# A linear-attention and GLU kernel: another hand-written order for its first stage, weight folds on halves of the array, and numerators that stand together

## The chip, the cores and the metric

The kernel runs on one core of one Trainium2 chip. The metric is the device time of one execution in microseconds (us). The five engines are named as in the profile: PE (matrix products; PEld is its weight loads), DVE, ACT and POOL (element-wise work), SP (which issues the DMA transfers).

## The reference

```python
xn = layernorm(x)                                   # x: 2048 x 1024, float32
q, k, v = split(xn @ wqkv)                          # 32 heads of 32
phi(t) = concat(softmax(t @ w_phi), softmax(-(t @ w_phi)))     # per head
num = phi(q) @ (phi(k).T @ v);  den = phi(q) @ sum(phi(k)) + 1e-6
s = concat_heads(num / den) @ wo
g = silu(((sigmoid(xn @ w_gate)) * (xn @ w_up)) @ w_down)      # inner width 3584
out = x + s * g
```

## The kernel before, in words

All large products are float32. An operand is split into a high and a low part, and a product is three matmuls of 128x128 by 128x512 (`mm3`, L224, L225, L226): high by high, high by low, low by high. Above that, each matrix product is cut into 2x2 blocks and made of seven block products, named B11, T2, T3, B21, T1, T4 and B22, whose operands are sums and differences of blocks. Those sums are made by POOL and DVE, the splits by ACT (the high part, L219 and L917) and DVE (the low part, L220 and L920), and PE is meant never to wait for them.

The tokens are worked in two halves of 1024. For each half come the projections V, K and Q (seven block products each; an `op` is one of them, four banks u of 48 matmuls in all), then 28 units of gate and up products (`glu`). Then follow the down projection (`dsteps`) and, for eight pairs of token tiles (`tp_`), the attention's output.

**The first stage** (L995, L996 and their neighbours) makes V for the first half. Its order is written by hand in the table `FIRST`: each entry is one small step, and `turn()` keeps each step behind the step ahead of it. `x0a`, `x0b`, `x1` and so on load a token tile; `bn`, `ag`, `add`, `sqrt`, `c`, `apply` are its layer norm; `T` transposes it on PE (L978); `V0a`, `r01` load weights; `xcast`, `xsub`, `wcast`, `wsub` are splits; `mm` are the matmuls (L996); `f` and `fc` are folds.

**A fold** multiplies the K or Q weights by `w_phi`, so that the projection gives t @ w_phi at once. There are eight groups, (K, 0) to (K, 3) and (Q, 0) to (Q, 3). A group loads four raw blocks n (`fold_load`, L323, 256 KB each), makes 16 matmuls with a block-diagonal `bd` (`fold_products`, L329, 128 rows by 128 columns, 128 columns moved; the profile has two records for each), copies the result out of the banks (`fold_copy`, L337 and L339), stores three of its blocks to `wf_d` (`fold_keep`, L350), loads the next group's raw blocks, and stores four sums. The first three groups stand in `FIRST`; the other five are in the queue `side`, and one is taken by `step()` after each bank u of the projections. The operands of the K and Q projections are read back from `wf_d` (L469, 1024 KB each).

**x tiles.** While the first half's gate products run, `x_task` prepares the second half's token tiles: it loads one, normalises it, stores it in pieces to `xs_d` (L665), loads it back in another order (L667), waits three steps (`yield`), transposes it on DVE (L672, which waits for that load) and, for every second tile, makes eight POOL pieces of sums (`x_sums`, L79). A step is one piece of background work, run after a block product.

**Numerators** (`numerators`, L832): for each pair `tp_`, 16 small matmuls of 64 columns and 256 moved columns, two records each, in two column halves of the array. They read `units_ph`, which DVE transposes (L817), and are called 13 products into the pair ahead.

Within an engine the framework's scheduler orders the instructions by its own estimate of times, unless `tc.issue_after(i)` puts an instruction behind another one. SP issues DMAs in order, and an SP instruction that waits holds up all that stand behind it.

Of the kernel before, what the change touches and what calls it, by code (L numbers as in the profile page):

```python
# [17 lines left out]
P = 128  # L18
# [14 lines left out]
class Ring:  # L33
# [3 lines left out]
    def next(self):  # L37
        self.n += 1
        return self.items[(self.n - 1) % len(self.items)]
# [56 lines left out]
x1, bn 1 0, x0a, bn 1 1, x0b, bn 0 0, wphi, x3, diag 1, ag 1, add 1, bn 0 1, sqrt 1, diag 0, ag 0, r01, add 0, c 1  # L96
0, sqrt 0, c 1 1, diag 2, c 1 2, r00, c 0 0, diag 3, c 0 1, c 0 2, c 0 3, V0a, f 0 1 3, c 0 4, c 0 5, apply 0 D, f 0
0 0, bn 3 0, r03, wcast B11 0, c 1 3, T 0 0 1, V0b, c 1 4, c 1 5, T 0 1 2, fc 0 1, wsub B11 0, xcast 0 0, fc 0 0,
r02, mm B11 0 0 a, xsub 0 0, xcast 0 1, f 0 3 3, V1b, apply 1 D, wcast B11 1, xsub 0 1, T 1 0 0, copy 0 0, V1a, mm
B11 0 0 b, bn 3 1, wcast B21 1, wsub B11 1, T 1 1 1, x2, copy 0 1, mm B11 0 1 a, xcast 1 1, ag 3, mm B11 0 1 b, copy  # L100
1 1, V2, bn 2 0, copy 1 0, f 0 2 2, bn 2 1, xcast 1 0, ag 2, mm B11 1 0 a, xsub 1 0, add 23, mm B11 1 0 b, xsub 1 1,
sqrt 23, wcast B21 0, x4, c 23 0, c 23 1, mm B11 1 1 a, c 23 2, c 23 3, evac B11 0, mm B11 1 1 b, c 23 4, c 23 5,
wsub B21 0, apply 2 A, x5, mm B21 0 0 a, bn 4 0, fc 0 3, T 2 0 0, V3, evac B11 1, T 2 1 1, bn 4 1, mm B21 0 0 b,
apply 3 A, ag 4, wsub B21 1, mm B21 1 0 a, xcast 2 1, mm B21 1 0 b, xcast 2 0, v 3 0 0 P, x6, copy 2 0, xsub 2 0, T
3 1 3, v 3 0 1 P, mm B11 2 0 a, bn 5 1, xcast 3 1, x7, mm B11 2 0 b, v 3 0 2 P, xsub 2 1, copy 2 1, v 3 0 3 P, fc 0
2, bn 6 0, mm B11 2 1 a, r10, mm B11 2 1 b, bn 7 1, v 3 1 0 P, r11, bn 5 0, v 3 1 1 P, T 3 0 2, kp 0, mm B21 0 1 a,
ag 5, xcast 3 0, v 3 1 2 P, bn 6 1, mm B21 1 1 a, copy 3 1, f 1 0 0, ag 6, xsub 3 0, v 3 1 3 P, f 1 1 1, r12, xsub 3
1, k 0 0 P, fc 1 0, bn 7 0, r13, k 0 1 P, mm B21 0 1 b, r20, ag 7, add 4567, mm B11 3 0 a, sqrt 4567, copy 3 0, mm
B11 3 0 b, c 4567 0, c 4567 1, v 2 0 0 D, evac B21 0, c 4567 2, c 4567 3, mm B21 1 1 b, c 4567 4, c 4567 5, apply 4
D, apply 7 A, mm B11 3 1 a, v 2 0 1 D, T 4 1 3, v 2 0 2 D, evac B11 2, v 2 0 3 D, T 4 0 2, v 2 1 0 D, copy 4 1, mm  # L110
B11 3 1 b, v 2 1 1 D, copy 4 0, apply 5 D, evac B21 1, f 1 3 3, xT3 0 0 D, fc 1 1, xT3 0 1 D, xT2 0 0 D, f 1 2 2,
evac B11 3, xT2 0 1 D, scast t3 0, xT4 0 0 D, xT4 0 1 D, T 5 0 0, fc 1 3, ssub t3 0, T 5 1 1, apply 6 A, kp 1, mm
B21 3 0 a, v 2 1 2 D, v 2 1 3 D, mm B21 2 0 a, v 0 0 0 D, v 0 0 1 D, copy 5 0, mm B21 2 0 b, k 0 2 D, copy 5 1, v 0
0 2 D, v 0 0 3 D, vst 3, mm B21 2 1 a, fc 1 2, v 0 1 0 D, T 6 1 1, k 0 3 D, scast t2 0, v 0 1 1 D, T 6 0 0, v 0 1 2
D, copy 6 1, mm B21 3 0 b, v 0 1 3 D, copy 6 0, xT3 1 0 D, xT3 1 1 D, wcast T2 1, T 7 0 2, xT3 2 0 D, xT3 2 1 D,
r21, mm B21 3 1 a, xT2 2 0 D, scast t3 1, mm B21 2 1 b, ssub t2 0, r22, wcast T2 0, v 1 0 0 D, r23, f 2 0 0, xT2 2 1
D, ssub t3 1, evac B21 2, vst 0, mm T2 0 0 a, scast t2 2, k 0 4 D, T 7 1 3, k 0 5 D, wsub T2 0, mm B21 3 1 b, copy 7
1, f 2 3 3, v 1 0 1 D, ssub t2 2, f 2 1 1, xT2 1 0 D, xT2 1 1 D, v 1 0 2 D, copy 7 0, mm T2 2 0 a, v 1 0 3 D, wcast
T3 0, v 1 1 0 D, mm T2 2 0 b, xT3 3 0 D, xT3 3 1 D, xT2 3 0 D, mm T2 2 1 a, scast t3 3, xT4 1 0 D, mm T2 0 0 b,
scast t2 1, xT2 3 1 D, v 1 1 1 D, scast t2 3, xT4 1 1 D, f 2 2 2, wsub T2 1, evac B21 3, scast t3 2, mm T2 0 1 a, fc  # L120
2 2, ssub t2 3, mm T2 3 0 a, fc 2 3, mm T2 2 1 b, ssub t2 1, fc 2 0, ssub t3 2, wcast T3 1, mm T2 3 0 b, k 1 0 D,
xT4 3 0 D, mm T2 0 1 b, scast t4 0, v 1 1 2 D, v 1 1 3 D, fc 2 1, wsub T3 0, V4, mm T2 3 1 a, scast t4 1, mm T2 1 0
a, mm T2 1 0 b, k 1 1 D, xT4 2 0 P, evac T2 2, mm T2 1 1 a, ssub t3 3, mm T2 3 1 b, k 1 2 D, ssub t4 1, mm T3 2 0 a,
k 0 6 P, evac T2 3, mm T2 1 1 b, xT1 1 0 D, mm T3 2 0 b, xT1 0 0 D, k 1 3 D, kp 2, wcast T4 0, k 1 4 D, mm T3 3 0 a,
xT4 3 1 D, xT4 2 1 P, evac T2 0, mm T3 3 0 b, wsub T3 1, scast t4 2, mm T3 2 1 a, vst 2, wcast T4 1, mm T3 0 0 a, k
# [5 lines left out]
D, mm T4 1 1 a, ssub b22 1, mm T4 2 0 b, xT1 0 1 D, scast t1 0, mm T4 2 1 a, wcast T1 1, mm T4 3 0 b, ssub t1 0, k 2  # L131
2 D, mm T4 3 1 a, scast t1 1, k 2 3 D, k 2 4 D, mm T4 2 1 b, scast t1 2, wsub T1 1, scast t1 3, mm T4 3 1 b, k 2 5
D, k 2 6 D, mm T4 1 1 b, ssub t1 2, k 2 7 D, ssub t1 3, ks 2, evac T4 3, ssub t1 1, wsub T1 0, evac T4 1, evac T4 2,
evac T4 0
"""


@with_exitstack
def hedgehog_glu_kernel(
# [74 lines left out]
    def pair(i):  # L214
        return slots[i][:, 0], slots[i][:, 1]
# [1206 lines left out]
```

## Time and profile before

| | |
|---|---|
| median of 3 runs (lowest, highest) | 2351.0 us (2350.98, 2352.16) |
| the profiled execution, and its span | 2350.23 us, 2348.5 us |
| busy: PE, DVE, ACT, POOL | 2331.4, 1624.6, 957.5, 1160.7 us |
| matmul records | 10644 |
| moved by DMA | 624.11 MB, mean 266 GB/s |

The span runs from the first to the last instruction. A matmul's own time (0.39 us for 512 columns) is longer than the step from one to the next (0.23 us), since matmuls overlap; so time is read here from start to start. In a row of a timeline the first number is the start, the second how long the merged row lasts, and what stands in brackets at the end is the idle time ahead of it, with what ended it.

### The profile page before, as it was taken

The numbers are of one execution on the slowest core, as the hardware profiler recorded it, in microseconds if no ns is written. First come the engines' busy times: TensorE is split into PE (matmuls) and PEld (weight loads), VectorE is DVE, ScalarE is ACT, GpSimd is POOL, SyncE is SP. The second block draws the span as 40 slices with busy tenths as digits, with TensorE's granted clock in tenths as the row PEclk, the third lists the DMA queues.
The fourth block names the chain that finished last, engine by engine and source line by source line (L and its number), as shares of the span: only waits on it lengthen the run. The fifth ranks groups of instructions, "written<-read, shape, count | busy, mean of one in ns | idle before, by whom it ended". The sixth has DMA issues, their size and how long they took to land.

```text
span 2348.5 us, 32142 instructions
## 1 busy us (share of the span) xinstructions
PE 2331.4 (99%) x10644; PEld 1922.2 (82%) x10644; DVE 1624.6 (69%) x2306; ACT 957.5 (41%) x1410; POOL 1160.7 (49%) x1320
## 2 busy tenths in 40 slices
PE   9999999999999999999999999999999999999999
PEld 7888888878888888888888888888888888887777
DVE  8734788677777675466867777866666777657655
ACT  7333354445454454233435344433434333344322
POOL 3210267677686642304363544555444455623777
PEclk9999999999999999999999999999999999999999
DMA  8875566888888889858888887879777877878774
GB/s 289 298 266 188 188 213 223 278 291 300 304 309 294 281 300 362 303 186 281 270 274 284 281 270 262 287 249 344 245 235 258 276 240 232 285 261 296 241 226 162
DMA packets 265415, 624.11 MB, mean 266 GB/s; under 512 B 36896, under 2 KB 65696, under 8 KB 260640
## 3 DMA queue, kind: packets, MB, share of 16 engines
q1 hardware_dynamic: 265248, 622.05, 78.0%
q8 instruction: 84, 1.38, 0.2%
q14 instruction: 83, 0.68, 0.1%
HBM read 373.42 MB, written 248.51 MB: 265 GB/s over the span
## 4 chain that ended last, share of the span: by engine, by line
PE 90%; DMA 4%; DVE 4%; issue 1%; ACT 1%; POOL 0%; SPq 0%; DVEq 0%; ACTq 0%
PE bank L224 29%; PE bank L225 29%; PE bank L226 29%; DMA fa<-w_down 2%; PE bank L602 1%; PE bank L832 1%; PE bank L329 1%; DMA x<-xk 1%; DVE x L920 1%; DMA fc<-xs_d 0%; DVE x L220 0%; DVE w L220 0%; DMA fa<-wv 0%; DVE w L920 0%; DMA wf_d<-x 0%
## 5 line engine op out<-in xcount | busy, mean ns | idle before, releaser
L225 PE MATMUL bank<-x,w 128*128 128x512 f32 x2352 | 916.4, 390 | 0.7 <-DVE x L220 0.7
L224 PE MATMUL bank<-x,w 128*128 128x512 f32 x2352 | 906.3, 390 | 3.7 <-DVE fc L1171 2.1
L226 PE MATMUL bank<-x,w 128*128 128x512 f32 x2352 | 905.9, 389 | 0.0
L79 POOL TENSOR_TENSOR fc<-fc 128x256 f32<-128x256 f32 x488 | 427.4, 907 | 480.0 <-DMA fc<-e_d 131.6
L220 DVE TENSOR_TENSOR w<-fa,w 128x512 fp32r<-128x512 f32 (+1 forms) x436 | 397.6, 915 | 201.3 <-ACT w L219 191.6
L219 ACT CAST w<-fa 128x512 fp32r<-128x512 f32 (+1 forms) x436 | 300.3, 691 | 556.8 <-PE bank L225 354.5
L224 PEld LDWEIGHTS bank<-x,w 128*128 128x128 f32 x2352 | 441.9, 188 | 97.1 <-DVE fc L1171 2.7
L225 PEld LDWEIGHTS bank<-x,w 128*128 128x128 f32 x2352 | 442.0, 188 | 92.7 <-DVE x L220 1.9
L226 PEld LDWEIGHTS bank<-x,w 128*128 128x128 f32 x2352 | 441.8, 188 | 91.8
L224 PE MATMUL bank<-w,x 128*128 128x512 f32 x636 | 248.4, 391 | 0.3 <-DVE fc L506 0.3
L225 PE MATMUL bank<-w,x 128*128 128x512 f32 x636 | 247.9, 390 | 0.0
L226 PE MATMUL bank<-w,x 128*128 128x512 f32 x636 | 247.4, 389 | 0.0
L79 POOL TENSOR_TENSOR fb<-fa 128x256 f32<-128x256 f32 x112 | 97.9, 894 | 218.6 <-PE bank L226 110.9
L79 POOL TENSOR_TENSOR fb<-fb,fc 128x256 f32<-128x256 f32 x132 | 123.6, 957 | 121.8 <-DVE fc L1188 121.6
L79 POOL TENSOR_TENSOR fc<-fc,sa 128x256 f32<-128x256 f32 x128 | 97.0, 788 | 93.5 <-issue 85.0
L224 PEld LDWEIGHTS bank<-w,x 128*128 128x128 f32 x636 | 119.4, 188 | 26.9 <-issue 1.9
L226 PEld LDWEIGHTS bank<-w,x 128*128 128x128 f32 x636 | 119.4, 188 | 24.8
L225 PEld LDWEIGHTS bank<-w,x 128*128 128x128 f32 x636 | 119.4, 188 | 24.3
L219 ACT CAST p<-fc 128x512 fp32r<-128x512 f32 x96 | 73.0, 764 | 131.2 <-DVE fc L575 79.0
L220 DVE TENSOR_TENSOR x<-fa,x 128x512 fp32r<-128x512 f32 x112 | 93.9, 839 | 45.0 <-ACT x L219 45.0
L219 ACT CAST w<-fb 128x512 fp32r<-128x512 f32 x112 | 69.0, 617 | 118.2 <-PE bank L225 86.4
L1188 DVE TENSOR_TENSOR fc<-fc,bank 128x512 f32<-128x512 f32 x84 | 57.5, 684 | 83.5 <-PE bank L226 61.6
(208 smaller groups left out, 2824.3 us busy)
## 6 DMA issues: line engine op xcount, KB each, us to landing
ws_d<-w SPq DMA_DIRECT2D x112, 512.0 KB, 4.2
w<-ws_d SPq DMA_DIRECT2D x112, 512.0 KB, 5.2
fa<-w_gu SPq DMA_DIRECT2D x84, 512.0 KB, 4.8
fa<-h_d SPq DMA_DIRECT2D x84, 512.0 KB, 4.9
fa<-wf_d SPq DMA_DIRECT2D x32, 1024.0 KB, 6.1
h_d<-fc SPq DMA_DIRECT2D x120, 256.0 KB, 4.7
fa<-w_down SPq DMA_DIRECT2D x80, 256.0 KB, 5.2
h_d<-fb SPq DMA_DIRECT2D x76, 256.0 KB, 4.5
```

Source lines behind the costliest of these rows:

```text
L79: last = self.engine.tensor_tensor(o[:, s], a[:, s], b[:, s], op=op)
L219: nc.scalar.copy(o[0], src)
L220: return nc.vector.tensor_sub(o[1], src, o[0].bitcast(F32))
L224: nc.tensor.matmul(o, a[0], b[0], start=first, stop=False, **kw)
L225: nc.tensor.matmul(o, a[0], b[1], start=False, stop=False, **kw)
L226: nc.tensor.matmul(o, a[1], b[0], start=False, stop=last, **kw)
L329: nc.tensor.matmul(ps[:, gs], r[:, gs], bd[:, 4 * (n // 2) + g], start=True, stop=True)
L602: nc.tensor.matmul(kvb[g // 2][:, g % 2 * 256:g % 2 * 256 + 256], v[:, g].rearrange("p a f -> p (a f)"), ph[:, g].rearrange("p a f -> p (a ...
L832: nc.tensor.matmul(ps[bs, j * 256:(j + 1) * 256], kv[:, 2 * j + b, bs], ph[:, 2 * j + b], start=True, stop=True, skip_group_check=True)
L920: nc.vector.tensor_sub(o[1], src, o[0].bitcast(F32))
L1188: v = nc.vector.tensor_add(b, u2 if q == 3 else u1, bank)
```

## The change

1. `FIRST` is another table: the tile x0 is loaded first, in halves, ahead of x1, and the steps behind it stand in another order.
2. `mm3` returns its last matmul. A list `last_mm` holds the last matmul of a row of them; the matmuls of the projections and of the attention's output, the later folds and the numerators are put behind it with `tc.issue_after`, so that they stand in the order of the code.
3. The five later fold groups are made by `fold_group`: the 128 rows are cut in two halves of 64, each half a matmul of its own (64 rows by 128 columns, 64 columns moved), alternately into two banks. They are copied by `fold_out`. The raw blocks of (K, 3) are loaded ahead of the loop over the operations, those of (Q, 0) by the fold of (K, 3). In `side` one or two empty steps stand ahead of each fold.
4. The 16 matmuls of `numerators` stand together.
5. `x_task` waits five steps in place of three, and counts 10 steps in place of 8.

```diff
 FIRST = """
-x1, bn 1 0, x0a, bn 1 1, x0b, bn 0 0, wphi, x3, diag 1, ag 1, add 1, bn 0 1, sqrt 1, diag 0, ag 0, r01, add 0, c 1
...
+x0a, x0b, bn 0 0, r02, bn 0 1, ag 0, x1, add 0, sqrt 0, c 0 0, c 0 1, c 0 2, c 0 3, r00, bn 1 0, c 0 4, wphi, bn 1
...
-        nc.tensor.matmul(o, a[1], b[0], start=False, stop=last, **kw)
+        return nc.tensor.matmul(o, a[1], b[0], start=False, stop=last, **kw)
...
+    def fold_group(which, k):
+        with tc.issue_after(last_mm[0]):
+            for n in range(4):
+                if n % 2 == 0:
+                    ps = [tps.next() for _ in range(2)]
+                r = folds.pop((which, k, n))
+                for g in range(4):
+                    for half in range(2):
+                        rs = slice(64 * half, 64 * half + 64)
+                        o = ps[half][:, n % 2 * 256:n % 2 * 256 + 256]
...
+                        m = nc.tensor.matmul(o, r[rs, g * P:(g + 1) * P], bd[rs, 4 * (n // 2) + g, rs], start=True, stop=True,
+                                             skip_group_check=True)
+                if n % 2:
+                    fold_out(which, k, n // 2, ps)
+        last_mm[:] = [m.ins]
...
-        for n in range(4):
-            fold_copy(which, k, n, fold_products(which, k, n, tps.next()))
+        fblock[which].next()
+        fold_group(which, k)
         fold_keep(which, k, False)
-        if k < 3:
+        if (which, k) != (Q, 3):
             for n in range(4):
-                fold_load(which, k + 1, n)
+                fold_load(*((which, k + 1) if k < 3 else (Q, 0)), n)
...
-        yield
-        yield
-        yield
+        for _ in range(5):
+            yield
...
+        with tc.issue_after(last_mm[0]):
+            for hb in range(2):
...
+                            m = nc.tensor.matmul(ps[bs, j * 256:(j + 1) * 256], kv[:, 2 * j + b, bs], ph[:, 2 * j + b],
+                                                 start=True, stop=True, skip_group_check=True)
...
+        last_mm[:] = [m.ins]
...
-    for w, k in [(K, 3)] + [(Q, k) for k in range(4)]:
+    for w, k, waits in ((K, 3, 2), (Q, 0, 1), (Q, 1, 2), (Q, 2, 2), (Q, 3, 2)):
+        side.extend([lambda: None] * waits)
         side.append(lambda w=w, k=k: fold(w, k))
+    for n in range(4):
+        fold_load(K, 3, n)
...
-    xs = [(8, lambda t=t: x_task(t)) for t in (CTT + 4 * a + q for q in range(4) for a in range(2))]
+    xs = [(10, lambda t=t: x_task(t)) for t in (CTT + 4 * a + q for q in range(4) for a in range(2))]
```

What it moves shows in the order of the built programs (line numbers of the changed kernel are larger by 3 to 47). First PE, in the middle of the attention's output: L832, in the changed kernel L867, are numerators, the rest products of three matmuls. Of one pair's 16, before, five stand at one place:

```order
L226 MATMUL bank_104<-x_0_90,fa_16054 128x512
L832 MATMUL bank_98<-fb_14626,p_14625 64x256 x4
L832 MATMUL bank_99<-fb_14626,p_14625 64x256
L224 MATMUL bank_102<-x_1_771,fa_16054 128x512
L225 MATMUL bank_102<-x_1_771,fa_16054 128x512
```

and eleven stand 51 matmuls later:

```order
L832 MATMUL bank_99<-fb_14626,p_14625 64x256 x3
L832 MATMUL bank_100<-fb_14626,p_14625 64x256 x4
L832 MATMUL bank_101<-fb_14626,p_14625 64x256 x4
L224 MATMUL bank_102<-w_93,x_1_611 128x512
L225 MATMUL bank_102<-w_93,x_1_611 128x512
```

After:

```order
L229 MATMUL bank_102<-w_93,x_0_91 128x512
L867 MATMUL bank_98<-fb_14710,p_14709 64x256 x4
L867 MATMUL bank_99<-fb_14710,p_14709 64x256 x4
L867 MATMUL bank_100<-fb_14710,p_14709 64x256 x4
L867 MATMUL bank_101<-fb_14710,p_14709 64x256 x4
L227 MATMUL bank_102<-w_93,x_0_91 128x512
```

So the five went to the place of the eleven. Pairs 4 to 8 stood as shown (five and eleven), pair 3 as one and fifteen, pair 2 as one, ten and five; each is one piece now. The first pair stands in three pieces, before and after.

Next SP's queue where the first stage ends. L323 (now L326) loads a raw block of a fold, L350 (now L385) stores a folded block, L469 (now L504) reads an operand of the K projection back, L503 (now L538) stores V. Before:

```order
L323 DMA fc_97<-wqkT 128x512
L323 DMA fb_96<-wqkT 128x512
L503 DMA qkv_d<-fc_97 128x512
L350 DMA wf_d<-fc_97 128x512 x2
L469 DMA fa_95<-wf_d 128x2048
L323 DMA fc_97<-wqkT 128x512
L350 DMA wf_d<-fc_97 128x512
L503 DMA qkv_d<-fc_97 128x512
L469 DMA fa_95<-wf_d 128x2048
```

After:

```order
L326 DMA fb_96<-wqkT 128x512 x2
L385 DMA wf_d<-fc_97 128x512 x2
L326 DMA fc_97<-wqkT 128x512
L504 DMA fa_95<-wf_d 128x2048 x2
L326 DMA fc_97<-wqkT 128x512
L385 DMA wf_d<-fc_97 128x512
```

The four L326 here are the raw blocks of (Q, 0). Both L504 now stand ahead of the last of them, and they wait for the landing of the two L385 above them, which are the folded blocks of (K, 3).

Last POOL, in the second unit of the gate products. `fc_97<-fc_97` are first the sums of the second x tile, and at the end (x2) a gate's product; `fa_95` are sums of the next unit's weights. Before:

```order
L79 TENSOR_TENSOR fc_97<-fc_97 128x256 x7
L79 TENSOR_TENSOR fb_96<-fa_95 128x256 x2
L79 TENSOR_TENSOR fc_97<-fc_97 128x256
L79 TENSOR_TENSOR fb_96<-fb_96,fa_95 128x256
L79 TENSOR_TENSOR fb_96<-fa_95 128x256
L79 TENSOR_TENSOR fb_96<-fb_96,fa_95 128x256
L79 TENSOR_TENSOR fb_96<-fa_95 128x256
L79 TENSOR_TENSOR fc_97<-fc_97 128x256 x2
```

After:

```order
L82 TENSOR_TENSOR fc_97<-fc_97 128x256 x6
L82 TENSOR_TENSOR fb_96<-fa_95 128x256 x2
L82 TENSOR_TENSOR fc_97<-fc_97 128x256 x2
L82 TENSOR_TENSOR fb_96<-fb_96,fa_95 128x256 x2
L82 TENSOR_TENSOR fc_97<-fc_97 128x256 x2
L82 TENSOR_TENSOR fb_96<-fa_95 128x256 x2
```

The gate's product stands two pieces further ahead. DVE's transpose of that x tile (L672, now L706) stands where it stood, behind the same bank's evacuation (L1169, now L1213).

127 lines of the change are left out of this document (74 added, 53 removed).

## The prediction

> **What bounds the kernel now.** I read the page first, then the busy time by stages, then the places where PE stands still.
>
> ```profile
> span 2348.5 us, 32142 instructions
> PE 2331.4 (99%) x10644; PEld 1922.2 (82%) x10644; DVE 1624.6 (69%) x2306; ACT 957.5 (41%) x1410; POOL 1160.7 (49%) x1320
> ...
> PE 90%; DMA 4%; DVE 4%; issue 1%; ACT 1%; POOL 0%; SPq 0%; DVEq 0%; ACTq 0%
> ```
>
> PE bounds it, and only two things can shorten the run: PE time per product, and the few places where PE waits. By stages (the first two numbers are a stage's length and PE's busy time in it):
>
> ```profile
> 0.00:20.00 20.00, 16.60 (x107) 15.27 (x107) 12.98 (x33) 10.74 (x20) 2.51 (x10) 1.00 0.94 334
> ...
> 60.00:80.00 20.00, 18.75 (x95) 15.73 (x94) 14.95 (x21) 5.04 (x8) 6.73 (x3) 1.00 0.91 325
> 80.00:100.00 20.00, 18.34 (x100) 15.49 (x100) 17.43 (x25) 9.65 (x17) 0.00 (x0) 1.00 0.64 213
> ...
> 440.00:500.00 60.00, 56.32 (x244) 45.52 (x243) 42.23 (x68) 23.82 (x35) 44.61 (x55) 0.99 0.82 276
> 500.00:2125.00 1625.00, 1625.00 (x7261) 1348.74 (x7261) 1147.27 (x1632) 675.97 (x982) 812.78 (x920) 1.00 0.82 277
> 2125.00:2348.00 223.00, 217.16 (x1045) 164.71 (x1043) 131.10 (x189) 66.76 (x115) 145.30 (x178) 1.00 0.70 231
> ```
>
> From 500 to 2125 us nothing is idle, and the change leaves the products there alone. What it can win or lose lies in the first 150 us, around 440 to 500, and after 2125. Its parts, by size:
>
> **Numerators in one piece.** Three pieces of the numerators, each between the last full matmul ahead and the first behind:
>
> ```profile
> 2170.17 0.39 PE L226 MATMUL bank<-w,x 128*128 128x512 f32 x1
> 2170.49 1.51 PE L832 MATMUL bank<-fb,p 128*64 128x256 f32 x10
> 2171.93 0.50 PE L224 MATMUL bank<-w,x 128*128 128x512 f32 x1
> 2172.26 0.39 PE L225 MATMUL bank<-w,x 128*128 128x512 f32 x1
> ...
> 2311.11 0.39 PE L226 MATMUL bank<-w,fa 128*128 128x512 f32 x1
> 2311.43 2.80 PE L832 MATMUL bank<-fb,p 128*64 128x256 f32 x22
> 2314.17 0.50 PE L224 MATMUL bank<-w,fa 128*128 128x512 f32 x1
> ...
> 2158.79 0.39 PE L226 MATMUL bank<-x,w 128*128 128x512 f32 x1
> 2159.11 2.38 PE L832 MATMUL bank<-fb,p 128*64 128x256 f32 x20
> 2161.42 0.50 PE L224 MATMUL bank<-x,x 128*128 128x512 f32 x1
> ```
>
> From full matmul to full matmul 10 records take 1.76 us, 22 take 3.06, 20 take 2.63. A record costs (3.06 - 1.76) / 12 = 0.108. A fixed cost is left beside the ordinary step of 0.23: 0.45 for 10 and for 22, 0.24 for 20. To each 0.10 is added, since the step behind a piece is 0.33 and not 0.23. So a piece costs 0.55 if its count of matmuls is odd (one is left without a partner in the other half), 0.34 if it is even. Before, six pairs have two odd pieces (1.10) and the second pair has odd, even, odd (1.44); after, each of the seven has one even piece. Sum: 6 x 0.76 + 1.10 = 5.7 us less. The piece stands where the later part stood, so what reads it is no later, and DVE's transposes for it were done by then. Bounds: 5.2 if the second pair's small piece costs less than this, 6.3 with a wait in that pair that may go too. **-5.7.**
>
> **Folds on halves of the rows.** One stretch of folds now, and the weight loads of both kinds:
>
> ```profile
> 134.15 1.05 PE L329 MATMUL bank<-fb,fc 128*128 128x128 f32 x8
> 135.04 1.95 PE L329 MATMUL bank<-fb 128*128 128x128 f32 x16
> 136.75 0.48 PE L225 MATMUL bank<-w,x 128*128 128x512 f32 x1
> ...
> L832 PEld LDWEIGHTS bank<-fb,p 128*64 128x64 f32 x256 | 18.6, 136 | 15.0 <-issue 5.6 <-DVE fb L817 1.6
> L329 PEld LDWEIGHTS bank<-fb 128*128 128x128 f32 x128 | 15.8, 191 | 2.2 <-issue 1.6
> ```
>
> 24 records take 2.60 us, 0.108 each, so a group of 32 takes 3.5. After, it has 64 records in 32 pairs. Each moves half the columns, but still loads 128 columns of weights. Column halves work side by side: 256 loads of 0.136 would be 34.8 us, and they cover 18.6. No row shows halves of the rows. A load's price is in the rows: 64 columns more cost 0.191 - 0.136 = 0.055, so 128 columns cost 0.11. That is what a fold record takes now, whichever of load and columns moved sets it. If the two halves' loads run side by side, as the column halves' do, a pair takes 0.11 and a group the same 3.5 as now. Halved price would be 0.054, serial loads 0.216: bounds of -8.6 and +17.3 for 160 pairs. I take the middle, since the loads' row is the nearest. Each group also enters and leaves the divided array, at the 0.34 of an even piece: five times. **+1.7.**
>
> [...]
>
> **The seam behind the first stage.** PE's three waits there:
>
> ```profile
> 78.40 1.13 PE L329 MATMUL bank<-fb 128*128 128x128 f32 x8 [1.25 <-DMA fb<-wqkT]
> ...
> 92.63 0.50 PE L224 MATMUL bank<-w,x 128*128 128x512 f32 x1 [0.34 <-DVE fc L506]
> 94.45 1.13 PE L329 MATMUL bank<-fb,fc 128*128 128x128 f32 x8 [1.32 <-DMA fc<-wqkT]
> ```
>
> With the 0.16 by which a matmul's own time exceeds the step, these are 1.4 + 0.5 + 1.5 = 3.4 us. Two are folds whose raw block had not landed. Now (K, 3) is loaded earlier and folded three banks later. **-3.4.** Behind it comes a new wait: the last raw block of (Q, 0) is queued on SP behind two 1024 KB reads that wait for stores to land.
>
> ```profile
> wf_d<-fc SPq DMA_DIRECT2D x3, 256.0 KB, 2.6
> ...
> GB/s 0 0 331 106 24 382 348 120 246 396 410 318 253 335 403 311 137 270 372 457 369 321 382 352 444 382 376 434 427 345 413 386 417 396 413 406 403 410 396 420
> ...
> wf_d<-fc SPq DMA_DIRECT2D x12, 256.0 KB, 6.1
> ```
>
> Count from the start of group (K, 3). It ends at 3.8. Two banks follow, 24 x 0.227 = 5.4; (Q, 0) starts at 9.3 and needs its last block at 12.1. The first half of (K, 3) is multiplied at 1.9, and copied and stored from 3.4 (estimated). The store lands 2.6 later (88 to 91 us, queue empty), at 6.0; the reads are issued then, the block's load at 7.0. The reads' 2.1 MB at some 410 GB/s take 5.1, behind 2.0 of delay, and the block 0.65: 13.8, a wait of 1.7. With a landing of 6.1 (88 to 112 us) it is 5.2; if the queue is faster, none. Late behind this wait on SP are the stores of V and (K, 3)'s other blocks, whose readers have ten us. I take the short landing, as the store follows a stretch in which SP itself waits. **+1.7.**
>
> **The x tiles.** What happens around the second tile:
>
> ```profile
> 471.68 1.31 DVE L672 STREAM_TRANSPOSE fc<-fc 128x512 f32<-128x512 f32 x2 [3.67 <-DMA fc<-xs_d]
> ...
> 486.92 0.69 DVE L1188 TENSOR_TENSOR fc<-fc,bank 128x512 f32<-128x512 f32 x1 [4.78 <-POOL fc L79]
> ...
> 487.76 0.47 PE L224 MATMUL bank<-x,w 128*128 128x512 f32 x1 [1.46 <-DVE fc L1188]
> ...
> 498.31 0.50 PE L224 MATMUL bank<-x,w 128*128 128x512 f32 x1 [2.12 <-DVE fc L1171]
> ...
> 498.00:502.00 4.00, 3.69 (x10) 2.93 (x11) 2.37 (x5) 2.02 (x4) 2.70 (x5) 0.61 1.05 246
> ```
>
> DVE waits 3.67 for the transpose's load; POOL's sums start late, its gate product too, then DVE, then PE: 1.6, later 2.3, and then a granted clock of 0.61 over four us, 1.6 more. But in the order the second tile's transpose has not moved against the products, so it waits for its load still. What moves is POOL's gate product, two pieces of some 0.73 earlier: 1.5 of the first wait of 1.6 goes. Of the second I let 0.4 go, and a quarter of the slow clock's 1.6, 0.4; with 0.2 for work DVE now does while it waits, 2.5. Ends: 0 (POOL is as late as ever) and 5.5 (all of it goes). Two more steps a tile are two empty calls. **-2.5.**
>
> **The start.**
>
> ```profile
> 4.42 1.88 DVE L950 BATCH_NORM_STATS2 norm<-x 128x6 f32<-128x512 f32 x3 [4.42 <-DMA x<-xk]
> ...
> 11.42 1.04 ACT L917 CAST w<-fa 128x1024 fp32r<-128x1024 f32 x1 [2.72 <-DMA fa<-wv]
> ...
> 13.49 0.73 PE L996 MATMUL bank<-w,x 128*128 128x512 f32 x2 [0.97 <-ACT x L917]
> ```
>
> 512 KB fewer stand ahead of the first weights: at 334 GB/s 1.6 us, so the first product starts near 11.9 and not 13.49. But one fold of eight records (0.9) ahead of it is put off, and the next fold's raw block r03, behind 4.2 MB, lands at about 15.5, where PE may wait up to 0.8. **-0.6**, between -2.5 and +2 for the rest of the table, whose waits are small now.
>
> **Sum:** -5.7 + 1.7 - 3.4 + 1.7 - 2.5 - 0.6 = -8.8. From the profiled execution's 2350.2 (span 2348.5 and 1.7 around it) that is 2341.4; the median of the runs lies 0.8 higher, so I predict 2342.2.
>
> **The rivals.** *Halves one after the other.* If the row halves' loads queue, a pair takes 0.216 and the folds cost 17.3 more: 2359.5, slower. It decides from 0.163 a pair on (8.8 / 160 = 0.055 above 0.108), where the change is even. For it: no row shows row halves side by side. Against it: the column halves' loads, which overlap.
>
> *Halves in half the time.* If the columns moved set a fold record's price, a pair takes 0.054: 8.6 less, 2333.6. Against it stands the load's 0.11. [...]
>
> *The late raw block.* If the stores land in 6.1 and the group behind has such a wait too, the seam gives back 3.5 to 6: about 2347, no change that can be measured.
>
> **How the numbers follow.** A measurement of this kernel tells a change from none at about 0.2%, 4.7 us: below 2346.3 is faster, above 2355.7 slower. The forecast (2337 to 2346) has 0.55, half the time 0.14, one after the other 0.14, the late block 0.17. Faster: 0.55 + 0.14 + a third of 0.17 = 0.75; same 0.11; slower 0.14. The range of 2332 to 2348 leaves out the serial halves and little else.
>
> **What would show it.** Right: seven pieces of 32 numerator records at 3.9 us from full matmul to full matmul; fold groups near 3.8; one wait for a raw block in (Q, 0), no wait at 92 to 95; DVE still waiting for the second transpose, with one PE wait behind it. Fold groups of 2 or 7 us make a rival right. A new wait of PE in the attention's output, now that its matmuls stand in the order of the code, would make all of it wrong.

## The result, and the profile after

The changed kernel takes 2385.8 us (median of 4 runs, 2382.6 to 2389.2), the kernel before 2351.0 beside it: a ratio of 1.0150 [1.0138, 1.0162], 35 us slower where 9 us faster was forecast. The profiled execution after has 2382.6 us and a span of 2380.8. Numbers worked out from many rows compare the start of the same full matmul (128x512, the first product being number 0) in two traces; that difference is called the lag. It belongs to the two executions that were profiled, while the ratios further down go by all runs. An evacuation is the reading of a finished bank by DVE or ACT; the matmul that fills that bank anew waits for it (1.13 us at 2258.02, further down).

| full matmul | place | lag of the changed kernel, us |
|---|---|---|
| 239 | end of the first stage | -0.9 |
| 480 | past the last fold | +33.1 |
| 1790 | before the second x tile | +32.8 |
| 2100 | behind it | +28.2 |
| 3600 | gate and up products | +31.5 |
| last | attention's output | +32.1 |

So nearly all is lost between 60 and 200 us, where the end of the first stage, the seam behind it and the folds are. The page, the stages (length, busy time of PE, PEld, DVE, ACT and POOL, then PEclk) and the list of PE's waits (us in all, how many, the longest):

```profile
span 2380.8 us, 32464 instructions
PE 2342.4 (98%) x10804; PEld 1931.5 (81%) x10804; DVE 1622.2 (68%) x2305; ACT 956.6 (40%) x1410; POOL 1165.5 (49%) x1326
```
```profile
60.00:80.00 20.00, 17.68 (x70) 13.79 (x69) 18.39 (x23) 4.03 (x6) 8.21 (x7) 0.91 0.66 224
80.00:100.00 20.00, 13.64 (x55) 10.88 (x54) 15.81 (x22) 7.79 (x12) 2.42 (x2) 0.83 0.41 136
100.00:150.00 50.00, 44.59 (x314) 37.76 (x313) 12.62 (x16) 11.60 (x18) 6.66 (x8) 0.86 0.69 240
150.00:200.00 50.00, 44.58 (x261) 36.49 (x260) 14.50 (x17) 14.11 (x21) 12.18 (x12) 0.86 0.66 220
440.00:500.00 60.00, 60.00 (x270) 49.85 (x269) 40.75 (x66) 26.88 (x42) 42.21 (x48) 1.00 0.83 276
```
```profile
PE bank L359 <- DMA fc<-wqkT: 6.5, 3, 4.2
PE bank L228 <- DVE w L956: 6.4, 1, 6.4
PE bank L227 <- DVE fc L1433: 5.6, 5, 1.1
...
PE bank L1032 <- DVE fc L541: 2.2, 1, 2.2
PE bank L227 <- ACT fc L547: 2.1, 1, 2.1
...
PE bank L359 <- DMA fb<-wqkT: 1.2, 1, 1.2
...
PE bank L227 <- DVE fc L541: 1.0, 1, 1.0
```

Without L1433, which belongs to the attention's output, these waits all lie between 60 and 200 us: 6.5 + 6.4 + 2.2 + 2.1 + 1.2 + 1.0 = 19.4. The granted clock takes nearly as much again: 9% of 17.7, 17% of 13.6 and 14% of twice 44.6 are about 16 us. Before, that clock was 1.00 there, and three waits made 2.9. 19.4 + 16 - 2.9 = 32.5, most of the 35.4 us by which the lag grows there (from -2.2 at matmul 140, 63 us, to +33.2).

A fold group itself costs what was forecast. (K, 3) and, with a late block, (Q, 0) and (Q, 1):

```profile
106.39 2.00 PE L359 MATMUL bank<-fb 64*128 64x64 f32 x32
108.22 1.95 PE L359 MATMUL bank<-fb,fc 64*128 64x64 f32 x32
```
```profile
115.77 2.00 PE L359 MATMUL bank<-fb 64*128 64x64 f32 x32
117.61 1.06 PE L359 MATMUL bank<-fb,fc 64*128 64x64 f32 x16
122.88 1.98 PE L359 MATMUL bank<-fb,fc 64*128 64x64 f32 x16 [4.21 <-DMA fc<-wqkT]
```
```profile
134.23 2.00 PE L359 MATMUL bank<-fb 64*128 64x64 f32 x32
137.44 3.68 PE L359 MATMUL bank<-fb,fc 64*128 64x64 f32 x32 [1.20 <-DMA fc<-wqkT]
```

64 records take 3.7 us. The 16 behind the wait of 4.21 take 1.98, twice the 1.06 of the 16 ahead of it, and the 32 behind the wait of 1.20 take 3.68 in place of 1.95: half speed. So that wait of 1.20 cost 1.73 us more in the group itself. The late block of (Q, 0) is the one that was foretold, on SP behind the two reads:

```profile
112.59 0.84 SPq L504 DMA_DIRECT2D fa<-wf_d  x2
113.53 0.38 SPq L326 DMA_DIRECT2D fc<-wqkT  x1
114.00 0.66 SPq L385 DMA_DIRECT2D wf_d<-fc  x1
```

What stands behind it was not foretold. The last row is the store of a block of (K, 3), queued behind the same reads. On DVE, the first of a group's sums (L82) overwrites the block that this store reads, and so must wait until it has landed: (K, 3)'s sum comes at 123.27, and that of (Q, 0), 12.47 us late, at 138.71, with the evacuation of a product's bank (L541) queued behind it:

```profile
123.27 0.69 DVE L82 TENSOR_TENSOR fc<-fc 128x512 f32<-128x512 f32 x1 [1.77 <-DMA wf_d<-fc]
...
125.55 0.69 DVE L82 TENSOR_TENSOR fc<-fc 128x512 f32<-128x512 f32 x1 [0.99 <-POOL fc L82]
138.71 0.69 DVE L82 TENSOR_TENSOR fc<-fc 128x512 f32<-128x512 f32 x1 [12.47 <-DMA wf_d<-fc]
139.32 0.68 DVE L541 TENSOR_TENSOR fc<-fc,bank 128x512 f32<-128x512 f32 x1
```

That evacuation holds up nothing on PE here, which is in a fold group. What does harm is SP: the stores of the sums must wait for the sums, and the next group's raw blocks stand among and behind them. Those of (Q, 2) are issued from 145.02 us on, and PE waits for two of them:

```profile
153.21 1.11 PE L359 MATMUL bank<-fb 64*128 64x64 f32 x16 [1.24 <-DMA fb<-wqkT]
155.43 3.68 PE L359 MATMUL bank<-fb,fc 64*128 64x64 f32 x32 [1.11 <-DMA fc<-wqkT]
```

Ahead of all that, at the first stage's end, PE stands 6.36 us for a split that DVE, busy since 90.3 without a pause, comes to last:

```profile
96.89 0.79 PE L228 MATMUL bank<-w,x 128*128 128x512 f32 x1 [6.36 <-DVE w L956]
```
```profile
92.75 2.35 DVE L223 TENSOR_TENSOR w<-fa,w 128x1024 fp32r<-128x1024 f32 x2
95.02 0.68 DVE L541 TENSOR_TENSOR fc<-fc,bank 128x512 f32<-128x512 f32 x1
95.62 1.22 DVE L956 TENSOR_TENSOR w<-p,w 128x1024 fp32r<-128x1024 f32 x1
```

In the attention's output a numerators' piece is 3.60 us from its first record to the next matmul (3.92 from the full matmul ahead), and about 7.4 us behind the piece a new wait stands, in five of the pairs; 12.5 us lie from the piece's start to the matmul that waited:

```profile
2245.52 3.67 PE L867 MATMUL bank<-fb,p 128*64 128x256 f32 x32
```
```profile
2258.02 0.50 PE L227 MATMUL bank<-x,fa 128*128 128x512 f32 x1 [1.13 <-DVE fc L1433]
```

### The profile page after: what moved, and what is told of

Its sections match the earlier page's. It is cut to its first block, busy times and chain, and to the rows that moved or that the text cites. A ratio compares the mean times of both kernels' runs of the same rounds, so it can differ in the third digit from the quotient of the medians.

```text
span 2380.8 us, 32464 instructions
## 1 busy us (share of the span) xinstructions
PE 2342.4 (98%) x10804; PEld 1931.5 (81%) x10804; DVE 1622.2 (68%) x2305; ACT 956.6 (40%) x1410; POOL 1165.5 (49%) x1326
## 4 chain that ended last, share of the span: by engine, by line
PE 84%; DVE 3%; issue 2%; DMA 2%; POOL 2%; ACT 0%; DVEq 0%; POOLq 0%; ACTq 0%
PE bank L227 27%; PE bank L228 27%; PE bank L229 27%; PE bank L637 1%; POOL fc L82 1%; DMA fc<-f_d 1%; DVE fb L851 1%; POOL fb L82 1%; PE bank L867 0%; DVE x L223 0%; DMA fc<-g_d 0%; DVE w L223 0%; DMA h_d<-fb 0%; POOL x L82 0%; DMA p<-qkv_d 0%
## 5 line engine op out<-in xcount | busy, mean ns | idle before, releaser
L82 POOL TENSOR_TENSOR fc<-fc 128x256 f32<-128x256 f32 x492 | 432.8, 910 | 503.8 <-DMA fc<-e_d 109.1
L228 PE MATMUL bank<-w,x 128*128 128x512 f32 x636 | 250.9, 394 | 6.4 <-DVE w L956 6.4
L227 PE MATMUL bank<-w,x 128*128 128x512 f32 x636 | 252.4, 397 | 3.1 <-ACT fc L547 2.1
L229 PE MATMUL bank<-w,x 128*128 128x512 f32 x636 | 250.1, 393 | 0.0
L82 POOL TENSOR_TENSOR fb<-fa 128x256 f32<-128x256 f32 x112 | 99.5, 909 | 211.1 <-DMA fa<-w_gu 118.3
L82 POOL TENSOR_TENSOR fb<-fb,fc 128x256 f32<-128x256 f32 x132 | 123.4, 955 | 119.2 <-DVE fc L1232 116.6
L228 PEld LDWEIGHTS bank<-w,x 128*128 128x128 f32 x636 | 121.6, 191 | 31.7 <-DVE w L956 6.8
L227 PEld LDWEIGHTS bank<-w,x 128*128 128x128 f32 x636 | 121.3, 191 | 31.7 <-ACT fc L547 2.5
L82 POOL TENSOR_TENSOR fc<-fc,sa 128x256 f32<-128x256 f32 x128 | 96.5, 785 | 99.7 <-issue 91.1
L229 PEld LDWEIGHTS bank<-w,x 128*128 128x128 f32 x636 | 121.3, 191 | 25.8
L223 DVE TENSOR_TENSOR p<-fc,p 128x512 fp32r<-128x512 f32 x96 | 97.3, 1018 | 32.4 <-ACT p L222 32.3
```

The source lines that it names most:

```text
L82: last = self.engine.tensor_tensor(o[:, s], a[:, s], b[:, s], op=op)
L223: return nc.vector.tensor_sub(o[1], src, o[0].bitcast(F32))
L227: nc.tensor.matmul(o, a[0], b[0], start=first, stop=False, **kw)
L228: nc.tensor.matmul(o, a[0], b[1], start=False, stop=False, **kw)
L229: return nc.tensor.matmul(o, a[1], b[0], start=False, stop=last, **kw)
```

## The experiments

"Pinned" means put behind an instruction with `tc.issue_after`, "free" means left to the framework's scheduler, which some expectations call the planner. First theory: the new table ends late on DVE (12 us with the clock), and the folds' blocks are late on SP for reasons of their own. Ratios are to the kernel before, run beside each; one thousandth is 2.35 us.

| kernel | median, us | ratio [95%] |
|---|---|---|
| changed | 2385.8 | 1.0150 [1.0138, 1.0162] |
| changed, old table | 2391.2 | 1.0183 [1.0166, 1.0200] |
| before, new table | 2351.2 | 1.0010 [1.0001, 1.0019] |
| before, (K, 3) late | 2354.1 | 1.0018 [1.0008, 1.0027] |
| before, numerators pinned | 2352.0 | 1.0015 [1.0006, 1.0025] |
| changed, free output | 2380.1 | 1.0128 [1.0115, 1.0141] |
| before, numerators together, free output | 2344.8 | 0.9976 [0.9966, 0.9985] |
| changed, whole rows | 2364.2 | 1.0071 [1.0056, 1.0086] |
| changed, folds free | 2374.3 | 1.0102 [1.0087, 1.0117] |
| changed, reads behind raw blocks | 2391.3 | 1.0176 [1.0163, 1.0189] |
| changed, sums' stores later too | 2388.0 | 1.0160 [1.0147, 1.0174] |
| changed, raw blocks from ACT | 2383.7 | 1.0136 [1.0117, 1.0155] |
| changed, copied block by block | 2392.6 | 1.0175 [1.0150, 1.0200] |
| changed, groups spaced | 2377.8 | 1.0122 [1.0105, 1.0138] |
| changed, spaced, sums later | 2375.1 | 1.0107 [1.0089, 1.0125] |
| before, x tiles 5 steps | 2350.2 | 1.0002 [0.9994, 1.0011] |
| changed, x tiles 3 steps | 2388.0 | 1.0162 [1.0148, 1.0176] |
| before, numerators together, x tiles 4 steps | 2340.5 | 0.9964 [0.9951, 0.9977] |
| the same, raw blocks from ACT | 2341.1 | 0.9966 [0.9954, 0.9979] |

### The first stage's end

**The changed kernel with the old table.** The edit is the text of `FIRST`.

> The changed kernel with the first stage's table of before; all else as changed. Theory A (the new table itself is late: its last low-part split, wsub T1 0, stands behind two splits of the next product on DVE, and PE waits 6.4 us for it, 2.2 us some 24 us earlier, with some 3 us of slow clock behind both; the folds' waits are a thing of their own): 2386 - 12 = 2374 us, and the fold groups of Q still wait for raw blocks and still run at half clock. Theory B (the folds' blocks are late only because the new table's end is late): the waits in the folds go too, 2386 - 12 - 18 = 2356 us or less.

It is no faster than the changed kernel. The wait at the end of the first stage is 8.4 us with this table, and the folds wait as before. Theory A falls in its first half: the table is not what makes that end late. Among the pinned products the new table is even worth 7.8 us (1.0183 against 1.0150).

**The kernel before with the new table.**

> The kernel before with the new table alone; folds, x tiles and numerators as before. Theory A (the table is late by itself): 2351 + 9 to 12 = 2360 to 2363 us, with a wait of about 6 us at the end of the first stage. Rival (the table is good and it is the pinned products and folds behind it that make PE wait): 2347 to 2351 us, no such wait.

2.3 us slower (0.2 to 4.5 by the interval), with no wait over 2 us near 90 us. The first product starts at 11.9 us, as the prediction had it for the table (in the changed kernel's profiled execution it starts at 13.15), and the gain is gone by 112 us (lag +0.9).

**The kernel before with the fold of (K, 3) late.** `last_mm` here holds the last product's matmul.

```diff
+    side.extend([lambda: None] * 2)
     for w, k in [(K, 3)] + [(Q, k) for k in range(4)]:
...
+            if (which, k) == (K, 3):
+                behind.enter_context(tc.issue_after(last_mm[0]))
             for n in range(4):
```

> The kernel before, old table, whole rows, free products, with one edit: the fold of (K, 3) is put behind the third bank's products after the first stage, as in the changed kernel (two empty steps, and behind the last product). Theory P (this fold's matmuls had filled PE's time while DVE was still at the first stage's last splits; taken out, PE stands there and the fold is paid again behind): a wait of 3 to 6 us at about 90 us with some 1.6 us of slow clock, 2349 + 4 to 8 = 2353 to 2357 us. Rival (the wait of 6.4 us at that place in the changed kernel comes from its table or its halves): 2347 to 2351 us.

4.2 us slower by the ratio, 5.1 by the lag at matmul 480. PE's waits there, in this kernel:

```profile
91.91 0.47 PE L224 MATMUL bank<-w,x 128*128 128x512 f32 x1 [2.57 <-DVE fc L509]
93.55 0.80 PE L225 MATMUL bank<-w,x 128*128 128x512 f32 x1 [1.17 <-DVE w L923]
```

The wait is there with the old table, whole rows and free products: (K, 3)'s 3.5 us of matmuls had covered DVE's last work there, an evacuation (L509) and a split (L923). With the fold gone a wait of 2.2 us also comes into the first stage, at 80.8 us here and at 68.4 in the changed kernel; the new table alone has none. The changed kernel's 6.4 is longer; what the rest is made of was not tried.

### The numerators

**The kernel before, numerators in one piece, products of the output pinned in the code's order.**

> The kernel before with the numerators in one piece and the matmuls of the attention's output in the order of the code, alone. Theory (five of the sixteen numerators, and a product that the scheduler had moved, stood before where PE would else wait for DVE's evacuation of a bank; the new wait of 1.3 us a pair takes back what the pieces had cost): 2350 to 2352 us, with five waits of about 1.3 us for DVE. Rival (those waits come from the later stages being shifted in the changed kernel, not from the order): 2345 us, without them.

3 us slower by the medians, with the five waits (5.9 us in all). In the profiled execution, one of the fastest of its ten, the lag is 0.0 at the end: the waits took back what the pieces had won. The later start of that stage has nothing to do with them.

**The changed kernel with the output's products free.**

```diff
-                with tc.issue_after(last_mm[0]):
-                    m = mm3(ps, (o[0][:, k], o[1][:, k]), ...
+                m = mm3(ps, (o[0][:, k], o[1][:, k]), ...
                 last_mm[:] = [m.ins]
```

> The changed kernel with the matmuls of the attention's output free again, the numerators still in one piece behind the last of them. Theory (the five waits of 1.3 us stand where the second, smaller piece of numerators and a product moved by the scheduler had stood; with the products free a moved product covers part): 2386 - 3 to 6 = 2380 to 2383 us, with fewer of these waits. Rival (the product's order is nothing, only the small piece covered the wait): 2386 us, five waits of 1.3 us.

5.2 us less than the changed kernel by the ratios, and none of the five waits is left.

**The kernel before with the numerators in one piece and free products.**

> The kernel before with nothing but the numerators in one piece; the matmuls of the attention's output are left free, as before. Theory (it was the pinned order of the products, not the pieces, that let the five waits of 1.3 us appear): the waits stay away and the 5.7 us of the pieces are won: 2349 - 5 to 6 = 2343 to 2344 us. Rival (the pieces pay for a wait in any order): 2349 us.

5.6 us faster (3.5 to 8.0 by the interval), where the prediction had 5.7. This kernel and the one pinned differ by the pins alone, so it was the pins. The full matmuls behind the last pair's numerators, by bank, pinned:

```
bank_102 x9, bank_105 x12, bank_104 x12, bank_105 x12, bank_102 x12
```

and free, here as in the kernel before:

```
bank_102 x9, bank_105 x12, bank_104 x12, bank_102 x11, bank_105 x12
```

Pinned, bank 105 is wanted again after 12 matmuls, before DVE has emptied it; free, the scheduler puts eleven of another bank between (fourteen in the pairs ahead).

### The folds

**The changed kernel with whole-row folds.** `fold_products` and `fold_copy` again, in the same groups and places.

> The changed kernel with its five later fold groups made of whole 128-row matmuls again, at the same place, in the same groups, with the same raw blocks and pins; only the halves are undone. Theory C (what costs is the group pinned in the products' row with blocks that land late; the halves change nothing): 2385 us within 3, waits for raw blocks in Q0 to Q2 as in the changed kernel, and half clock behind them. [...] Theory E (half-row matmuls are slow themselves): 2365 us or less.

0.8% (18.6 us, also the difference of the spans) less than the changed kernel. This is theory E's number, not its mechanism: a group takes 3.49 us here and 3.72 in halves, 1.2 us for five. What goes are the waits. The fold stretch alone wins more than the total shows: from matmul 140 to 600 the lag grows by 11.7 us here and by 35.4 in the changed kernel, and 5.8 us of that difference are lost again in the output, with waits of 1.8 and 1.6 us that the changed kernel does not have. (Q, 0) and (Q, 1) here, and SP's raw blocks, all four ahead of the reads (L494):

```profile
114.31 1.95 PE L352 MATMUL bank<-fb 128*128 128x128 f32 x16
116.10 1.95 PE L352 MATMUL bank<-fb,fc 128*128 128x128 f32 x16
...
126.06 1.95 PE L352 MATMUL bank<-fb 128*128 128x128 f32 x16
127.84 1.95 PE L352 MATMUL bank<-fb,fc 128*128 128x128 f32 x16
```
```profile
106.61 0.38 SPq L326 DMA_DIRECT2D fb<-wqkT  x1
107.09 0.41 SPq L376 DMA_DIRECT2D wf_d<-fc  x1
107.59 0.38 SPq L326 DMA_DIRECT2D fb<-wqkT  x1
108.06 0.46 SPq L376 DMA_DIRECT2D wf_d<-fc  x1
108.61 0.90 SPq L326 DMA_DIRECT2D fc<-wqkT  x2
110.90 0.33 SPq L494 DMA_DIRECT2D fa<-wf_d  x1
```

New theory: the halves change the order that the scheduler gives to SP, ACT and DVE.

**The changed kernel with its folds free.** `fold_group` without `issue_after`.

> The changed kernel with the halves kept but the later fold groups no longer put behind the last product: the scheduler may place each fold matmul where it likes, as before the change. Theory F: some of the late blocks are covered, since other matmuls can stand ahead of a late block, and the fold of (K, 3) fills part of the 6.4 us wait at the first stage's end: 2370 to 2378 us. Theory H (it is the pins that cost, the halves nothing): 2360 us or less, near the kernel with whole-row folds or better. Theory G: 2385 us or more.

11 us less than the changed kernel, as theory F had it. (K, 3) goes back ahead of the first stage's end, and the 6.4 us there become 2.2; (Q, 1) still takes 8.8 us.

**The reads behind the raw blocks.**

```diff
+                    with ExitStack() as behind:
+                        if c == 0 and folds:
+                            behind.enter_context(tc.issue_after(last_sp[0]))
-                    nc.sync.dma_start(row4(r), wf_d[what, i])
+                        nc.sync.dma_start(row4(r), wf_d[what, i])
```

> The changed kernel, halves and groups kept, with each 1024 KB read of the folded weights put behind the last raw block of the next group in SP's queue. Theory F (the halves cost nothing on PE; they cost because a pair of blocks is copied out only when both are done, so that the planner puts reads and stores ahead of the raw blocks on SP, the blocks land late, and each such wait halves the clock): the 4.2 us wait of Q0 and most of the later ones go, groups of 3.7 us, 2386 - 15 to 20 = 2366 to 2371 us. Theory G (half-row matmuls themselves bring waits or a slow clock): 2380 us or more, groups over 6 us still.

(Q, 0) is on time, 3.72 us. (Q, 1) takes 8.5, (Q, 3) waits 5.4, and a product 6.5 for ACT: the kernel is 6 us slower than the changed one, and F falls as it stands.

**In addition the sums' stores a group later.**

```diff
+        with tc.issue_after(last_sp[0]):
+            while owed:
+                fold_keep(*owed.pop(), True)
...
-        with tc.issue_after(last_sp[0]):
-            fold_keep(which, k, True)
+        owed.append((which, k))
...
```

> The changed kernel with halves and groups kept; the reads stand behind the next group's raw blocks (as in the kernel before this one), and the four stores of a group's sums are put one group later, behind the raw blocks of the group after, about where SP has them in the kernel with whole-row folds. Theory F' (it is SP's order alone: stores that wait for DVE's sums stand ahead of raw blocks): no wait over 1 us in the groups, groups of 3.7 us, no slow clock between 105 and 165 us, 2386 - 18 to 22 = 2364 to 2368 us. Theory G (something else in the halves makes PE wait): waits of several us in the groups or right behind them as in the two kernels with this order half mended, 2380 us or more.

Three groups of 3.72, two of 5.6 and 4.7, but two products wait 3.6 for ACT's splits and 5.8 for ACT's copy. F' falls.

**The raw blocks from ACT.** `nc.scalar.dma_start` for those of Q.

> The changed kernel with halves and groups kept; only the raw blocks of Q's fold groups are issued from ACT's queue and no longer from SP's, so that no store or read that waits on SP can stand ahead of them. Theory F'' (the halves are innocent on PE; a raw block stands on SP behind whatever waits there, and the next group is late with it): waits for raw blocks under 1 us in all groups, groups of 3.7 us, full clock from 105 to 165 us, 2386 - 15 to 22 = 2364 to 2371 us. Theory G (the halves bring waits by another way): the waits stay or move to other places in the same stretch, 2380 us or more.

Again (Q, 0) is on time and (Q, 1) and (Q, 2) are not (6.9 and 11.4 us): the wait had moved to ACT's queue, which issues a raw block of (Q, 2) at 144.56 us, when that group has begun (144.00). F'' falls.

**Copied block by block.** This kernel puts the folded columns in another order than the projections need; the work is the same.

```diff
-                if n % 2:
-                    fold_out(which, k, n // 2, ps)
+                fold_out(which, k, n, ps)
```

> The changed kernel with halves kept, but each block is copied out of the banks as soon as it is multiplied (two small copies a block) and not two blocks at a time. Theory M (what the halves bring is that copies, stores and sums start a block later, and SP's order is planned around that): 2370 us or less, near the kernel with whole-row folds. Rival (the order on SP is another because the planner takes the halves' matmuls for something else than they are; when the copies start matters little): 2380 us or more, with waits of 4 us and more in the groups.

No gain, groups of 5.7, 7.9 and 9.6 us: theory M falls.

**The groups spaced.**

```diff
-    for w, k, waits in ((K, 3, 2), (Q, 0, 1), (Q, 1, 2), (Q, 2, 2), (Q, 3, 2)):
+    for w, k, waits in ((K, 3, 2), (Q, 0, 3), (Q, 1, 4), (Q, 2, 4), (Q, 3, 4)):
```

> The changed kernel, halves, groups and pins kept; only more empty steps stand between its fold groups (3, 4, 4 and 4 ahead of those of Q in place of 1, 2, 2, 2), so that 48 to 60 full matmuls stand between two groups and no longer 24 to 36. Theory O (with the halves one turn of raw block, product, copy, store, landing, sum, store takes some 15 to 18 us on the queues, where the old spacing allows 9 to 12; the wait only moves when one queue is mended): groups of 3.7 us without waits, 2386 - 15 to 22 = 2364 to 2371 us. Theory G (the halves bring waits at any spacing): 2380 us or more.

Some 7 us less than the changed kernel, between the two theories, and no fold waits for a raw block. In their place PE waits three times, 11.6 us, for DVE's evacuation of a bank. The longest, on DVE and on PE:

```profile
141.46 0.69 DVE L82 TENSOR_TENSOR fc<-fc 128x512 f32<-128x512 f32 x1 [12.70 <-DMA wf_d<-fc]
142.07 1.22 DVE L223 TENSOR_TENSOR w<-fa,w 128x1024 fp32r<-128x1024 f32 x1
143.21 0.68 DVE L541 TENSOR_TENSOR fc<-fc,bank 128x512 f32<-128x512 f32 x1
```
```profile
143.94 0.80 PE L227 MATMUL bank<-w,x 128*128 128x512 f32 x1 [7.48 <-DVE fc L541]
```

The sum's wait for the store's landing holds up the evacuation, and that holds up PE.

**Spaced, with the sums a group later.** Sums and their stores of a group are made in the next group's `fold`, behind the last evacuation; the last group has no next, so its own follow at once.

> The changed kernel with halves and groups, spaced as in the kernel with more empty steps between them (3, 4, 4, 4), and in addition the four sums of a group and their stores are made one group later, behind the last evacuation, so that a sum's wait for the landing of the store ahead of it is long over when DVE comes to it. Theory Q (what makes PE wait in the spaced kernel is DVE, which stands at a group's first sum for 10 to 12 us until that store has landed, with the evacuation of a product's bank queued behind it): the three waits of 3.8, 3.5 and 7.5 us for DVE's evacuation go, with their slow clock, 2378 - 12 to 20 = 2358 to 2366 us. Theory G (the halves make PE wait by something else): 2375 us or more, with waits in the same stretch.

2375 us: the rival's number, not the theory's 2358 to 2366, and the interval overlaps that of the kernel ahead. Yet the stages tell the theory from its rival:

```profile
105.00:188.00 83.00, 83.00 (x601) 70.26 (x600) 24.69 (x30) 23.79 (x36) 13.00 (x16) 1.00 0.78 267
188.00:205.00 17.00, 9.17 (x29) 7.01 (x28) 6.04 (x8) 4.32 (x6) 4.80 (x4) 0.70 0.42 130
```

In the first 83 us lie all five groups in halves, each of 3.72 us, and PE never stands still: G's mechanism falls. In the next 17 the one group whose sums were not put off does what the others did before:

```profile
195.73 0.69 DVE L82 TENSOR_TENSOR fc<-fc 128x512 f32<-128x512 f32 x1 [15.24 <-DMA wf_d<-fc]
196.34 0.68 DVE L545 TENSOR_TENSOR fb<-fc,bank 128x512 f32<-128x512 f32 x1
```
```profile
197.08 0.79 PE L227 MATMUL bank<-w,x 128*128 128x512 f32 x1 [7.83 <-DVE fb L545]
```

That wait and the slow clock behind it cost 10.9 us (lag +10.5 at matmul 520, +21.4 at 700). From matmul 140 to 600 the lag grows by 23.2 us here, by 28.4 in the kernel ahead and by 35.4 in the changed kernel; the total hides it, since this execution, the slowest of its four, loses 6.6 us in the output. DVE still stands at some of the sums that were put off, 5.95 us at 136.03 and 5.48 at 176.05, but PE waits for none of them.

So a group is a ring through four queues that are worked in order (SP's at 112.59 to 114.00 and DVE's at 138.71 and 139.32 in the changed kernel): raw block (SP), products (PE), copy (ACT), store and landing (SP), sum (DVE, POOL), store (SP), next raw block. In each kernel with halves some member of it still stood ahead of something that PE needed; where one queue was mended, the wait turned up in the next. With whole rows DVE waits at the sums too, 5.26 us at 137.15 and 6.40 at 153.02, but less long, and no evacuation is queued right behind. Why the scheduler's order for whole rows comes out so at the same spacing is open.

### The x tiles, and a faster version

**The kernel before with five empty steps.**

> The kernel before with nothing but the x tiles' longer wait (five empty steps, ten in all). Theory (the 5.2 us that the changed kernel is faster between 440 and 530 us come from this edit alone): 2349 - 5 = 2344 us, without the waits of 1.6 and 2.3 us and without the slow clock behind them. Rival (they come from the later start of everything in the changed kernel, against the loads): 2349 us.

No gain. In the profiled execution (2354.6 us, the second slowest of its twelve) the two waits go, but one of 4.9 us for DVE's L1170 comes at 493 us, with slow matmuls behind it, and 3.4 us more are lost in the units between matmuls 2100 and 3600. That later loss, 3.0 to 4.0 us, stands in all twelve traces with five steps; with three it is 0.0, with four 0.1 and 1.2.

**The changed kernel with three.**

> The changed kernel with the x tiles' old wait (three empty steps, eight in all). If the 5.2 us that it is faster around 440 to 530 us come from the longer wait: 2386 + 5 = 2391 us, with the waits of 1.6 and 2.3 us back. If they come from the later start of that stage against the loads: 2386 us within 2.

The waits come back and cost 4.7 us between matmuls 1790 and 2100, as the changed kernel had won, and 1.9 between 1700 and 1790; but the 3.3 us that the changed kernel loses in the later units, between 720 and 870 us, are gone. At the last matmul 3.2 us are left; by the ratios it is 2.8, and the intervals overlap.

**The kernel before, numerators in one piece, free output, four empty steps.**

> As the kernel with the numerators in one piece and free products, and the x tiles wait four empty steps in place of three (nine in all). If one step more moves POOL's gate product ahead of the second tile's sums and DVE's transpose does not stand in the way: 2343 - 3 to 5 = 2338 to 2340 us. If, as with five steps, another evacuation comes late in its place: 2343 to 2346 us.

8.5 us faster than the kernel before; in the profiled execution the lag falls by 4.6 us at the x tiles and by 5.1 in the output.

**The same with the later raw blocks from ACT.**

> The fastest so far (the kernel before with the numerators in one piece, free products and four empty steps) with the raw blocks of the later fold groups issued from ACT's queue. If SP's order is what makes the two folds wait 1.3 us each behind the first stage, those go: 2340 - 2 to 3 = 2338 us. If ACT, busy there with splits, issues them later than SP did: 2340 to 2346 us.

No further gain; the waits behind the first stage stay near 1 us each.

## Why the prediction was wrong

**Folds.** The price of half-row matmuls was right: 3.72 and 0.21 for entering and leaving, 3.93 a group where 3.84 was put. Whole rows take 3.58 by the same count, so five groups cost 1.7 us more, the forecast's term.

**The late raw block** was seen at its place, 4.2 us within the bounds of 0 to 5.2. The count's 2.0 of delay is an estimate: 2.6, the landing of 256 KB with the queue empty, less 0.65 for its bytes. In the changed kernel the two reads, issued from 112.59 on, landed 5.9 us after their issue (median), the block 9.3 after its own. The first step that failed is the sentence behind it: "Late behind this wait on SP are the stores of V and (K, 3)'s other blocks, whose readers have ten us." One of those stores is waited for by DVE before a sum may overwrite the block; behind the sum stand evacuations on DVE and sum stores on SP, and behind these the next raw blocks. The reader that counts is not the one that wants the data but the one that wants the buffer. The two kernels with spaced groups show it, with 7.48 and 7.83 us of PE behind 12.70 and 15.24 of DVE. The rival of the late block had the late blocks and stopped after the second group.

**The clock.** The prediction priced waits by their length. Between 60 and 200 us most of the waits were followed by half speed, some 16 us in all, nearly the other half of the loss; a wait of 1.20 us cost 1.73 more. It had the row for it (498 to 502 us, 0.61) and used it for the x tiles alone.

**The seam.** The waits of before went as forecast. What would be late next was asked for raw blocks and not for DVE. This second step that failed left out a wait of 6.36 us: the fold of (K, 3), moved three banks down, had been PE's work while DVE finished its evacuations and splits. Moving it alone costs 4 to 5 us.

**Numerators.** 5.7 us was right for the pieces: 3.92 us from full matmul to full matmul where 3.9 was put, and 5.6 us in the version with free products. The step that failed is that the new order of the output's products was named as a danger and given neither a price nor a chance: five waits of 1.1 us took all of it back (the lag grows by 0.6 us in the output).

**The x tiles.** The two waits went almost whole, 4.7 us where 2.5 was put. The step "so it waits for its load still" failed: the second tile's transpose waits 1.32 us (on DVE at 503 us) where it was 3.67. But 3.3 us come back later, in units that the prediction left out ("From 500 to 2125 us nothing is idle, and the change leaves the products there alone"); by the kernels with three, four and five steps this is the longer wait's own price. What in it makes the later units wait was not tried.

**The start** was a term of -0.6; the table alone costs 2.3 us in the kernel before and wins 7.8 among the pinned products.

## What to carry to other kernels

Before fixing an order that a scheduler had been free to choose, list what stood ahead of each matmul that can wait: pieces that look like overhead may be what covers a wait, and the gain of joining them was had here (5.6 us) only while the products around stayed free. When an in-place sum must wait for a store to land, what stands behind it on its engine waits too (12.70 us of DVE held up an evacuation, and that 7.48 us of PE), so put such a sum where the landing is past, or where nothing that PE needs is queued behind it. And where PE waits, look for half clock behind the wait and count that time too (behind the 2.08 us ahead of 187.00, seven matmuls at a step of 0.43 us in place of 0.23).

## What the runs showed of the hardware

**Half-row matmuls.** A pair of halves (64 rows, 128 columns of weights, 64 moved) takes 3.72 / 32 = 0.116 us where no block is late, a whole-row record (128 rows, 128 columns moved) as good as the same: 3.49 / 32 = 0.109. Moving half the columns won nothing. The weight loads, of halves (spaced, sums later) and of whole rows, take the same time each, 188 and 191 ns (the number ahead of the last bar), and the two loads of a pair start 7 ns apart (at 106.38 us, changed kernel).

```profile
L359 PEld LDWEIGHTS bank<-fb 64*128 64x128 f32 x160 | 9.3, 188 | 1.8 <-issue 1.8
```
```profile
L352 PEld LDWEIGHTS bank<-fb 128*128 128x128 f32 x80 | 9.7, 191 | 0.4
```

**The clock behind a wait.** Among full matmuls, these waits were followed by 5 to 8 matmuls at a step of 0.43 us in place of 0.23: 2.21 us ahead of 68.44, 6.36 ahead of 96.89 and 2.08 ahead of 187.00 (changed kernel), and 2.12 ahead of 498.31 (the kernel before). Behind single waits of 0.99 us (195.33) and 1.13 us (2258.02, both in the changed kernel) and of 1.46 us (487.76, the kernel before) the step was 0.23 but for the first, 0.31 to 0.34. In the half-row groups the clock fell behind a wait of 1.20 us (137.44, above). Whether that is due to the half rows was not tried apart.
